# A load moved behind two transposes, and another held until one of them has landed, in a linear-attention and feed-forward kernel

## The chip, the cores and the metric

The kernel runs on one core of a Trainium2 chip. The metric is the device time of one execution in microseconds (us). Before the change it is 257.47 us, the median of three runs (256.48 to 258.15).

The engines of the core are named as in the profile: PE (TensorE; PEld is its weight load), DVE (VectorE), ACT (ScalarE), POOL (GpSimd) and SP (SyncE). Each engine works through its own instructions in the order of the program. An instruction waits at its place for the semaphores that it needs, and everything behind it on the same engine waits with it. In this kernel SP and POOL hardly compute: they issue DMAs, SP the loads of whole blocks, the transposes and the stores, POOL the weights, some early loads and the short tails of q, k and v. An issue is not a landing: a DMA is handed to a queue, and lands when its data have been moved.

## The reference

The input is q, k and v with 8 batches, 8 heads, 576 positions and 64 dimensions, in f32, and the four matrices of a feed-forward part.

```python
def phi(x):
    return np.where(x > 0, x, np.exp(x) - 1.0) + 1.0
q_p, k_p = (phi(q), phi(k))
kv = np.einsum('bhsd,bhse->bhde', k_p, v)
z = np.sum(k_p, axis=2)
num = np.einsum('bhsd,bhde->bhse', q_p, kv)
den = np.einsum('bhsd,bhd->bhs', q_p, z)[..., None] + 1e-06
attn = (num / den).astype(np.float32)

x = attn.transpose(0, 2, 1, 3).reshape(B * S, H * D)     # 4608 x 512
a = x @ w1                                               # 512 x 1024
b = x @ w2                                               # 512 x 1024
h = a * b @ w3                                           # 1024 x 1024
out = h @ w_out                                          # 1024 x 512
```

## The kernel before, in words

The attention of a batch is worked in the 512 positions that make four tiles of 128 (`NJ = 4`) and a tail of 64 (`R`). Blocks of q, k and v of one batch are loaded in two halves of four heads each, 512 KB a half. The two last matrices are multiplied with each other at the start, into `wf_sb`, so that a batch's feed-forward part is two products with w1 and w2, an elementwise product, and one product with `wf_sb`.

The whole order of the work is written out by hand in a string, `ORDER`, that `step` reads token by token. A token is a letter, the batch, and a part; a `+` at its end chooses another engine. Those that matter here are:

- `L`, `M`, `N`: load half a block of k, q, v (`load_qkv`, line 105, on SP here). The blocks take turns in 13 buffers of one pool, in the order of the tokens. `R`: load the tails of q and k (part 0: four DMAs of 64 KB) or of v (part 1: two DMAs), line 114, on POOL with a `+`.
- `x`, `y`, `z` for k and `X`, `Y`, `Z` for q: the exponential on ACT (line 178), max(x, 0) + 1 on DVE (line 183) and the minimum of the two on DVE (lines 203 and 208), which is phi. The result for k is `kj`, for q `qj`, and both tails go behind `qj` in one tile.
- `v`: cast half a block of v (line 214) or its tail (line 220) to bf16, on ACT, DVE or POOL.
- `K`: `kv_full`, the products of phi(k) with v and with ones into `kvp` on PE (lines 238 to 248), copied to `kv` (line 253).
- `T`: `qt_load`, a DMA on SP that transposes all of a batch's phi(q) and its tails, 18 blocks of 128 x 128 (line 268).
- `A`: `nat`, the product of transposed phi(q) with kv on PE (line 299), and on DVE the division into `xn` (lines 303 to 305). `D`: `xt_load`, a DMA on SP that transposes a batch's `xn`, 16 blocks, into `xt` (line 330).
- `F`: `f_unit`, for one of eight column blocks the products of x with w1 and with w2 (line 341), copied out by ACT (line 346) and multiplied by DVE (line 347). They use four PSUM banks (`mm_ps`), two for a unit.
- `O`: `o_unit`, eight products with `wf_sb` (line 498) and a copy of the result (line 500). `S`: the store of two of them, 512 KB, on SP (line 508).

A number behind a letter is the batch and the part: `L4.0` is the first half of k of batch 4, `T3.0` the transpose of q of batch 3, `D2.0` that of x of batch 2, `K3` the k-v products of batch 3.

Batches overlap: while PE computes the feed-forward part of batch 2, the attention of batch 3 is made ready, and the blocks of batch 4 and 5 are loaded. The loads run far ahead of their use, and the queue of SP holds many of them at a time. A DMA on SP or POOL also waits for the landing of the DMA that is eight before it on the same engine, since eight semaphores take turns.

Loads can be ordered against one another by `GATES`, a string that is empty before the change. `step` keeps the last DMA of each load under its token in `held`, and a token that stands on the left of a `<` in `GATES` waits until the DMA held under the token on the right has landed (`loaded` and `after`):

```python
def loaded(s, ins):
    s = s.rstrip("+")
    if s in gates:
        after(ins, held[gates[s]])
    held[s] = ins
```

The functions that the diff touches, and what calls them:

Of the kernel before, what the change touches and what calls it, by code (L numbers as in the profile page):

```python
# [13 lines left out]
P = 128  # L14
# [6 lines left out]
def kernel(  # L21
# [11 lines left out]
    nc = tc.nc  # L33
# [58 lines left out]
    raw, held = {}, {}  # L92
# [16 lines left out]
    def load_tail(b, part, alt):  # L109
        names = ("qk", "v")[part]  # L110
        t = raw[names + "r", b] = ldr.tile([P, len(names), RW], F32, tag="ldr" + names, name=names + "32r")
        for i, name in enumerate(names):
            for g in range(2):
                ins = (nc.gpsimd if alt else nc.sync).dma_start(  # L114
                    out=t[g * R:(g + 1) * R, i].rearrange("p (h d) -> p h d", d=D),
                    in_=src[name][b, g * 4:(g + 1) * 4, NJ * P:S, :].rearrange("h p d -> p h d"))
        return ins

    WQ = 256

# [135 lines left out]
    NB = KC * NJ  # L256

    def qt_tile(b):
        if (b, 0) not in qts:
            t = qts[b] = att.tile([P, NB + 2, P], BF16, tag="qt", name="qt")  # L260
            qts[b, 0] = t[:, 0:NB].rearrange("p (c j) t -> p c (j t)", j=NJ)
            qts[b, 1] = t[:, NB:NB + 2]
        return qts[b]

    def qt_load(b, part):
        t, s = qt_tile(b), ph["qt", b]
        i = NB if part else 0
        nc.sync.dma_start(out=t[:, i:NB + 2], in_=s[:, i * P:(NB + 2) * P], transpose=True)

    def q_tr(b, g, alt):  # L270
        qj, _ = ph["q", b]
# [77 lines left out]
    def f_unit(c, f):  # L349
        a_ps, b_ps = f_open(c, f)  # L350
        for ps, w in ((a_ps, w1_sb), (b_ps, w2_sb)):
            for kc in range(KC):
                f_mm(c, f, ps, w, kc)
        f_close(c, f, a_ps, b_ps)
# [4 lines left out]
    def ws_make(w, i, alt):  # L359
        t, s = (w1_sb, w2_sb)[w], wss[w]  # L360
        s[i] = ws_p.tile([P, 2, NQ * P], BF16, tag=f"w{w}{i}", name=f"ws{w}{i}")

        def blk(r, h):
            return t[:, 2 * h:2 * h + 2, r * NCH:r * NCH + NQ * P]
        a, b, op = ((lambda: blk(1, 0), lambda: blk(1, 1), ALU.add),
                    (lambda: s[0], lambda: blk(0, 0), ALU.subtract),
                    (lambda: blk(0, 0), lambda: blk(1, 0), ALU.subtract),
                    (lambda: blk(0, 1), lambda: s[1], ALU.subtract))[i]
        (nc.gpsimd if alt else nc.vector).tensor_tensor(out=s[i], in0=a(), in1=b(), op=op)

    def xs_make(c, i, alt):
        if c not in xss:
            xss[c] = xt_p.tile([P, 4, 2, 2, P], BF16, tag="xs", name="xs", bufs=1)
        x, s = xt_of(c), xss[c]

        def blk(h, r):
            return x[:, 2 * r:2 * r + 2, 2 * h:2 * h + 2]
        a, b = ((lambda: blk(0, 1), lambda: blk(0, 0)), (lambda: blk(1, 1), lambda: s[:, 0]),
                (lambda: blk(1, 1), lambda: blk(0, 1)), (lambda: blk(1, 0), lambda: s[:, 1]))[i]
        (nc.gpsimd if alt else nc.vector).tensor_tensor(  # L380
            out=s[:, i], in0=a(), in1=b(), op=ALU.subtract)
# [19 lines left out]
    def g_unit(c, q, i):  # L401
        if c not in abs_:
            abs_[c] = ab_p.tile([P, FC, NCH], BF16, tag="ab", name="ab")
        st = cs_.setdefault((c, q), {})
        a, m, name, first = ((), ((0, 0, 0), (0, 0, 0), "u", True), ((0, 0, 1), (0, 1, 0), "t", True),
                             ((1, 1), (1, 1), "u", False), ((1, 0), (1, 0), "t2", True),
                             ((1, 2), (1, 2), "u", False), ((1, 3), (0, 1, 1), "t2", False),
                             ((0, 1, 1), (1, 3), "u", False))[i]
        if first:
            pool, tag = (o_ps_p, "ou"[q % 2]) if name == "u" else (mm_ps, "mm")  # L410
            st[name] = pool.tile([P, 2, HN], F32, tag=tag, name="g" + name)
        t = st[name]
        g_product(t, c, q, a, m, first)
        if i in (1, 3, 4):
            s = st["s", i] = fsm("gs")
            nc.scalar.copy(out=s, in_=t)
        elif i in (2, 5, 6):
            s = st["c", i] = fsm("gc")
            nc.vector.tensor_tensor(out=s, in0=st["s", {2: 1, 5: 4, 6: 3}[i]], in1=t, op=ALU.add)
        else:  # L420
            s = fsm("ga")
            nc.scalar.copy(out=s[:, 0], in_=t[:, 0])
            nc.vector.tensor_mul(out=abs_[c][:, q + 4, 0:HN], in0=s[:, 0], in1=t[:, 1])

    def g_mul(c, q, i, alt):
        s = cs_[c, q]["c", i]
        f, r = {2: (q, 0), 5: (q + 4, 1), 6: (q, 1)}[i]
        (nc.gpsimd if alt else nc.vector).tensor_mul(
            out=abs_[c][:, f, r * HN:(r + 1) * HN], in0=s[:, 0], in1=s[:, 1])
# [64 lines left out]
    def o_unit(c, m, alt):  # L494
        ab = abs_[c]
        o_ps = o_ps_p.tile([P, DM], F32, tag="ou"[m % 2], name="o_ps")
        for f in range(FC):
            nc.tensor.matmul(o_ps, ab[:, f, m * P:(m + 1) * P], wf_sb[:, f, :],  # L498
                             start=(f == 0), stop=(f == FC - 1))
        copy_of(alt)(out=rows_of(c, m // 2)[:, m % 2], in_=o_ps)  # L500
# [45 lines left out]
    R2.0+ h0 h1 A0.4 P1.1+ Y2.1 h2 h3 R3.0+ M3.1 i0 A1.4 M2.0 i1 x2.1 X3.1 Z2.1 F1.7 F1.6 x2.2 L2.0  # L546
    y2.1 y2.2 Y2.0 x3.2 R3.1+ X2.0 O0.3 N2.1 x2.0 z2.1 N2.0 y2.0 z2.2 Z2.0 F1.0 M3.0 R5.0+ y3.2 T2.0
    v2.1 L3.0 Y3.1 R2.1+ F1.5 N3.1 v2.0+ z2.0 L3.1 Z3.1 v2.2+ O0.2 F1.2 F1.1 Y3.0 y5.2 z3.2 K2 F1.4
    A2.2 X3.0 F1.3 L4.0 A2.3 x3.0 O0.1 Z3.0 A2.0 x3.1 N3.0 y3.0 O0.0 v3.1 S0.1 A2.1 y3.1 R5.1+ z3.0
    z3.1 v3.0 v3.2 O1.1+ O1.0 T3.0 D2.0 S0.0 K3 R4.1+ R4.0+ O1.3 A3.0 O1.2 A3.2 L4.1 v4.2+ F2.6 A3.3  # L550
    F2.3 N4.1 y4.1 F2.1 M4.0 x4.1 A3.1 x4.0 F2.0 M4.1 y4.2 M6.1 v5.2+ x4.2 F2.7 Y4.0 D3.0 F2.4 z4.1
    X4.1 F2.2 Y4.1 v4.1 S1.0 F2.5 Z4.1 M5.0 N4.0 X4.0 Z4.0 A3.4 z4.2 y4.0 O2.3 F3.7 M5.1 Y5.0 v4.0
    A2.4 F3.6 z4.0 L5.0 T4.0 R6.0+ x5.2 Y5.1 X5.0 F3.1 N5.1 Z5.0 S1.1 O2.2+ K4 F3.2 M6.0 x6.2 X5.1
# [8 lines left out]
    F7.7 F7.2 F8.0 S6.1 F8.7 S6.0 F8.1 F8.5 F7.4 F8.2 F8.4 F7.6 O8.2 F7.5 H8.2 F7.3 F7.0 O8.3 H8.3  # L562
    O7.0 O7.1 S7.0 O8.0 O8.1 S8.0 O7.2 H7.2 Q7.3
    """
    GATES = ""
    ctx.enter_context(tc.manual_schedule())
    gates = dict(g.split("<") for g in GATES.split())

# [6 lines left out]
    def step(s):  # L575
        alt = len(s) - len(s.rstrip("+"))
        op, *at = s.rstrip("+").replace(".", " ").split()
        b = int(op[1:]) if op[1:] else None
        i = int(at[0]) if at else None
        t = op[0]  # L580
        if t == "F":
            f_unit(b, i)
        elif t == "G":
            g_unit(b, i, int(at[1]))
        elif t == "m":
            g_mul(b, i, int(at[1]), alt)
        elif t == "e":
            ws_make(b, i, alt)
        elif t == "d":
            xs_make(b, i, alt)  # L590
        elif t == "O":
            o_unit(b, i, alt)
        elif t == "V":
            w_unit(b, i)
        elif t == "s":
            s_make(b, i, alt)
        elif t == "S":
            o_store(b, i)
        elif t == "H":
            o_store(b, i // 2, i % 2)  # L600
        elif t == "Q":
            o_last(b, i)
        elif t == "I":
            constants(b, alt)
        elif t == "w":
            w3_tr(b, alt)
        elif t == "u":
            wf_mm(b, i, alt)
        elif t == "t":
            wt_make(b)  # L610
        elif t in "LMN":
            name = "kqv"["LMN".index(t)]
            loaded(s, load_qkv(name, b, i, alt))
        elif t == "R":
            loaded(s, load_tail(b, i, alt))
        elif t == "B":
            loaded(s, load_w12(b, i))
        elif t == "C":
            loaded(s, load_wo(b))
        elif t == "E":  # L620
            loaded(s, load_w3(b))
        elif t in "xX":
            phi_exp("kq"["xX".index(t)], b, i)
        elif t in "yY":
            phi_max1("kq"["yY".index(t)], b, i, alt)
        elif t in "zZ":
            phi_min("kq"["zZ".index(t)], b, i)
        elif t == "v":
            v_unit(b, i, alt)
        elif t == "T":  # L630
            qt_load(b, i)
        elif t == "a":
            q_tr(b, i, alt)
        elif t == "K":
            kv_full(b, alt)
        elif t == "A":
            nat(b, i)
        elif t == "D":
            xt_load(b, i)
        elif t == "P":  # L640
            xt_tr(b, i, alt)
        elif t == "h":
            if b == 0:
                held["h"] = [f_open(0, 0), f_open(0, 1)]
            for f in range(2):
                for ps, w in zip(held["h"][f], (w1_sb, w2_sb)):
                    f_mm(0, f, ps, w, b)
        elif t == "i":
            f_close(0, b, *held["h"][b])
# [32 lines left out]
```

## Time and profile before

| What | us |
|---|---|
| median of three runs | 257.47 |
| the profiled execution | 255.3 |
| its span, from the first to the last instruction | 253.5 |
| PE busy in it | 231.9 |
| DVE busy | 156.9 |
| ACT busy | 116.3 |
| POOL busy | 48.9 |

The granted clock of TensorE is 0.997 of full speed over the span. The DMA engines are at or near full use in nearly all of the first two thirds of the span, and hardly used in most of the last third; 38.80 MB are read from HBM and 9.44 MB written.

The profile is one execution. Its span is shorter than the execution's own time by what lies before the first and after the last instruction. Times in the views are microseconds from the start of the span. In a timeline, a row gives the start, the length, the engine, the line, the operation, the tiles as out<-in, their shapes and the number of instructions merged; in brackets stands the idle time of the engine before it and what ended it. A `q` behind an engine's name is its sequencer, which issues a DMA: the length is that of the issue, not of the transfer. The times to landing come from the list of DMA issues.

### The profile page before, as it was taken

What the parts mean: (1) busy time and instruction counts of PE and PEld (TensorE: products, weight loads), DVE (VectorE), ACT (ScalarE), POOL (GpSimd) and SP (SyncE); (2) the same over time, 40 slices, a digit from 0 to 9 for tenths busy, and PEclk for the clock granted to TensorE, in tenths of its full rate; (3) what the DMA queues carried; (4) which work ended last, traced back from release to release, by engine and by line L of the source; (5) the groups of instructions that cost most, each with busy time, mean ns of one, the idle gap of its engine ahead of it and who ended that gap; (6) DMA issues with size and microseconds to landing.
All of it is one profiled execution on the core that took longest, in us unless ns stands there. A gap on an engine that the chain in (4) does not pass through costs nothing.

```text
span 253.5 us, 3863 instructions
## 1 busy us (share of the span) xinstructions
PE 231.9 (91%) x1400; PEld 118.1 (47%) x1400; DVE 156.9 (62%) x350; ACT 116.3 (46%) x179; POOL 48.9 (19%) x82
## 2 busy tenths in 40 slices
PE   0088999999999789999999999999999999999994
PEld 0064564654454444445445545454544444444442
DVE  0548498679988546897987899878235632442300
ACT  2402676357756518738472573645332322333231
POOL 8524469446154100600000000000000000000000
PEclk9999999999999999999999999999999999999998
DMA  6999999999999999899999989646611244000144
GB/s 213 216 226 217 293 271 182 194 278 296 279 253 284 243 244 354 182 299 238 346 295 257 299 214 269 155 92 151 204 23 67 98 84 168 0 0 0 41 147 145
DMA packets 65427, 49.54 MB, mean 195 GB/s; under 512 B 33536, under 2 KB 60416, under 8 KB 65408
## 3 DMA queue, kind: packets, MB, share of 16 engines
q1 hardware_dynamic: 54576, 37.10, 56.7%
q0 software_dynamic: 10688, 12.06, 23.7%
q8 instruction: 11, 0.18, 0.3%
q10 hardware_dynamic: 144, 0.13, 0.1%
q14 instruction: 8, 0.07, 0.1%
HBM read 38.80 MB, written 9.44 MB: 190 GB/s over the span
## 4 chain that ended last, share of the span: by engine, by line
PE 75%; DMA 20%; POOL 1%; issue 1%; ACT 1%; ACTq 0%; POOLq 0%
PE a_ps L341 24%; PE b_ps L341 24%; PE o_ps L498 20%; DMA w3b<-in_moe_w_dram 10%; DMA out_dram<-o_sb 5%; PE nd L299 3%; DMA qk32r<-in_k_dram 3%; DMA xt<-xn 2%; PE kvp L244 2%; PE o_ps L523 1%; PE kvp L248 1%; PE kvp L238 0%; POOL w3b L136 0%; ACT e L178 0%; PE xtp L320 0%
## 5 line engine op out<-in xcount | busy, mean ns | idle before, releaser
L341 PEld LDWEIGHTS <-w_sb 128*128 128x128 bf16 x576 | 55.2, 98 | 63.0 <-issue 1.6
L347 DVE TENSOR_TENSOR ab<-a_sb,b_ps 128x512 bf16<-128x512 f32 x72 | 49.3, 685 | 39.4 <-PE b_ps L341 31.1
L341 PE MATMUL a_ps<-xt,w_sb 128*128 128x512 bf16 x256 | 66.7, 379 | 1.4 <-DMA xt<-xn 0.8
L346 ACT COPY a_sb<-a_ps 128x512 f32<-128x512 f32 x72 | 41.9, 585 | 56.1 <-PE a_ps L341 51.7
L341 PE MATMUL b_ps<-xt,w_sb 128*128 128x512 bf16 x256 | 66.7, 379 | 0.0
L498 PE MATMUL o_ps<-wf_sb,ab 128*128 128x512 bf16 x280 | 64.4, 379 | 0.0
L498 PEld LDWEIGHTS <-ab 128*128 128x128 bf16 x280 | 26.8, 98 | 30.0
L500 ACT COPY o_sb<-o_ps 128x512 f32<-128x512 f32 x29 | 16.9, 585 | 40.6 <-PE o_ps L498 28.2
L305 DVE TENSOR_TENSOR xn<-nd,r 128x512 bf16<-128x512 f32 x32 | 22.1, 691 | 1.1
L178 ACT ACTIVATE e<-q 128x1024 bf16<-128x1024 f32 x16 | 16.7, 1054 | 6.2 <-DMA q<-in_q_dram 6.2
L178 ACT ACTIVATE e<-k 128x1024 bf16<-128x1024 f32 x16 | 16.6, 1055 | 5.3 <-DMA k<-in_k_dram 5.3
L146 PE MATMUL w3p<-ident,w3b 128*128 128x128 bf16 x64 | 5.7, 242 | 13.5 <-DMA w3b<-in_moe_w_dram 13.5
L299 PEld LDWEIGHTS <-qt 128*128 128x128 bf16 (+1 forms) x160 | 11.5, 99 | 11.4 <-issue 2.7
L183 DVE TENSOR_SCALAR y<-q 128x1024 bf16<-128x1024 f32 x16 | 11.1, 700 | 8.2 <-DMA q<-in_q_dram 8.2
L299 PE MATMUL nd<-kv,qt 128*128 128x130 bf16 (+1 forms) x160 | 15.8, 220 | 0.5 <-ACT kv L253 0.5
L153 PE MATMUL wf_ps<-wt_sb,w3t 128*128 128x512 bf16 x64 | 15.1, 379 | 0.6 <-DMA wt_sb<-in_moe_w_out_dram 0.6
L303 DVE TENSOR_SCALAR r<-nd 128x8 f32<-128x8 f32 (+1 forms) x40 | 6.4, 161 | 12.6 <-PE nd L299 12.2
L114 POOL DMA_DIRECT2D qk32r<-in_q_dram x14 | 9.3, 674 | 16.9 <-ACT a_sb L346 14.8
L208 DVE TENSOR_TENSOR qj<-e,y 128x512 bf16<-128x512 bf16 x32 | 11.9, 416 | 0.4 <-ACT e L178 0.3
L208 DVE TENSOR_TENSOR kj<-e,y 128x512 bf16<-128x512 bf16 x32 | 11.9, 417 | 0.2
L146 PEld LDWEIGHTS <-w3b 128*128 128x128 bf16 x64 | 4.5, 108 | 15.0 <-DMA w3b<-in_moe_w_dram 14.8
L114 POOL DMA_DIRECT2D v32r<-in_v_dram x12 | 7.6, 640 | 18.1 <-DVE vr L220 8.1
(59 smaller groups left out, 185.0 us busy)
## 6 DMA issues: line engine op xcount, KB each, us to landing
out_dram<-o_sb SPq DMA_DIRECT2D x15, 512.0 KB, 3.8
q<-in_q_dram SPq DMA_DIRECT2D x13, 512.0 KB, 7.9
k<-in_k_dram SPq DMA_DIRECT2D x13, 512.0 KB, 6.3
v<-in_v_dram SPq DMA_DIRECT2D x12, 512.0 KB, 8.9
w3b<-in_moe_w_dram POOLq DMA_DIRECT2D x8, 256.0 KB, 12.2
w_sb<-in_moe_w_dram POOLq DMA_DIRECT2D x8, 256.0 KB, 7.3
q<-in_q_dram POOLq DMA_DIRECT2D x3, 512.0 KB, 11.4
k<-in_k_dram POOLq DMA_DIRECT2D x3, 512.0 KB, 12.4
```

The source lines that it names most:

```text
L114: ins = (nc.gpsimd if alt else nc.sync).dma_start(out=t[g * R:(g + 1) * R, i].rearrange("p (h d) -> p h d", d=D), in_=src[name][b, g * 4:( ...
L153: nc.tensor.matmul(wfs[i], w3ts[i][:, kc, :], wo_sb[:, kc, :], start=(kc == 0), stop=(kc == FC - 1))
L178: nc.scalar.activation(out=e, in_=x, func=AF.Exp)
L183: (nc.gpsimd if alt else nc.vector).tensor_scalar(out=y, in0=x, scalar1=0.0, scalar2=1.0, op0=ALU.max, op1=ALU.add)
L208: nc.vector.tensor_tensor(out=p[0][:, 2 * g + c].rearrange("p j u d -> p u j d"), in0=e[:, c], in1=y[:, c], op=ALU.min)
L299: nc.tensor.matmul(nd[rows, g, i * 2 * E1:(i + 1) * 2 * E1], w, kvs[b % 2][:, i, g].rearrange("p u e -> p (u e)"), start=True, stop=True)
L305: nc.vector.tensor_tensor(out=dst.rearrange("p (g h) e -> p g h e", g=2), in0=v4[:, :, :, 0:D], in1=r[rows].unsqueeze(3).to_broadcast([n, ...
L341: nc.tensor.matmul(ps, w[:, kc, f * P:(f + 1) * P], xt_of(c)[:, :, kc, :], start=(kc == 0), stop=(kc == KC - 1))
L346: nc.scalar.copy(out=a_sb, in_=a_ps)
L347: nc.vector.tensor_mul(out=abs_[c][:, f, :], in0=a_sb, in1=b_ps)
L498: nc.tensor.matmul(o_ps, ab[:, f, m * P:(m + 1) * P], wf_sb[:, f, :], start=(f == 0), stop=(f == FC - 1))
L500: copy_of(alt)(out=rows_of(c, m // 2)[:, m % 2], in_=o_ps)
```

## The change

Three things change.

- In `ORDER`, `L4.0` moves from before `A2.3` to behind `S0.0`. On SP it is issued behind `N3.0`, `S0.1`, `T3.0`, `D2.0` and `S0.0` and not ahead of them. The other tokens keep their order; on PE, DVE, ACT and POOL no instruction moves. Since the buffers of blocks are given out in the order of the tokens, `L4.0` and `N3.0` exchange theirs.
- `GATES` holds one entry, `R6.0<T3.0`: the tails of q and k of batch 6, loaded on POOL, wait for the landing of the transpose of q of batch 3. For that `step` keeps the DMA that `qt_load` now returns.
- `load_tail` returns the first of its DMAs and no longer the last, so that a gate holds the first of them, and with it those behind it on the same engine.

```diff
@@ load_tail
         t = raw[names + "r", b] = ldr.tile([P, len(names), RW], F32, tag="ldr" + names, name=names + "32r")
+        first = None
         for i, name in enumerate(names):
             for g in range(2):
                 ins = (nc.gpsimd if alt else nc.sync).dma_start(
                     out=t[g * R:(g + 1) * R, i].rearrange("p (h d) -> p h d", d=D),
                     in_=src[name][b, g * 4:(g + 1) * 4, NJ * P:S, :].rearrange("h p d -> p h d"))
-        return ins
+                first = first or ins
+        return first
@@ qt_load
-        nc.sync.dma_start(out=t[:, i:NB + 2], in_=s[:, i * P:(NB + 2) * P], transpose=True)
+        return nc.sync.dma_start(out=t[:, i:NB + 2], in_=s[:, i * P:(NB + 2) * P], transpose=True)
@@ ORDER
-    A2.2 X3.0 F1.3 L4.0 A2.3 x3.0 O0.1 Z3.0 A2.0 x3.1 N3.0 y3.0 O0.0 v3.1 S0.1 A2.1 y3.1 R5.1+ z3.0
-    z3.1 v3.0 v3.2 O1.1+ O1.0 T3.0 D2.0 S0.0 K3 R4.1+ R4.0+ O1.3 A3.0 O1.2 A3.2 L4.1 v4.2+ F2.6 A3.3
+    A2.2 X3.0 F1.3 A2.3 x3.0 O0.1 Z3.0 A2.0 x3.1 N3.0 y3.0 O0.0 v3.1 S0.1 A2.1 y3.1 R5.1+ z3.0 z3.1
+    v3.0 v3.2 O1.1+ O1.0 T3.0 D2.0 S0.0 L4.0 K3 R4.1+ R4.0+ O1.3 A3.0 O1.2 A3.2 L4.1 v4.2+ F2.6 A3.3
@@
-    GATES = ""
+    GATES = "R6.0<T3.0"
@@ step
         elif t == "T":
-            qt_load(b, i)
+            held[s] = qt_load(b, i)
```

## The prediction

> **What bounds the kernel now.** I read the page's first two parts, then every idle stretch of PE in the timeline, then who ended it, and last the SP and POOL queues in front of those two places. PE is busy for 231.9 of 253.5 us:
>
> ```profile
> PE 231.9 (91%) x1400; PEld 118.1 (47%) x1400; DVE 156.9 (62%) x350; ACT 116.3 (46%) x179; POOL 48.9 (19%) x82
> ```
>
> Its idle time lies in the first 40.6 us, with two exceptions. The timeline of PE (start, length, instruction, idle time before it and its releaser in brackets):
>
> ```profile
> 83.78 1.89 PE L498 MATMUL o_ps<-wf_sb,ab 128*128 128x512 bf16 x8
> 87.10 0.61 PE L244 MATMUL kvp<-vt,kj 128*128 128x130 bf16 x8 [1.43 <-ACT vt L214]
> 87.84 0.27 PE L248 MATMUL kvp<-vr,qj 128*128 128x260 bf16 x1
> ...
> 93.37 1.02 PE L341 MATMUL a_ps<-xt,w_sb 128*128 128x512 bf16 x4 [0.79 <-DMA xt<-xn]
> ```
>
> The first is K3, which waits 1.43 us for batch 3's v, and 0.13 us more for its tail (87.10 + 0.61 = 87.71 to 87.84). The second is F2.6, which waits 0.79 us for D2.0, the transpose of batch 2's x. Together 2.35 us; after 93.4 PE never waits again, so whatever ends sooner there ends the kernel sooner, as long as nothing behind it becomes late.
>
> Who holds these two? ACT's timeline, and the chain that ended last (start, length, what; for a DMA from issue to landing):
>
> ```profile
> 82.51 1.05 ACT L214 CAST vt<-v 128x1024 bf16<-128x1024 f32 x1
> 86.00 1.05 ACT L214 CAST vt<-v 128x1024 bf16<-128x1024 f32 x1 [2.43 <-DMA v<-in_v_dram]
> ```
>
> ```profile
> 74.23 13.31 DMA out_dram<-o_sb
> 87.53 5.79 DMA xt<-xn
> ```
>
> ACT casts one half of v at 82.51 and then waits 2.43 us for the other half, N3.0. The store S0.1, ready at 74.23, lands only at 87.6: the queue is backed up. SP's timeline shows in which order:
>
> ```profile
> 72.24 1.00 SPq L105 DMA_DIRECT2D k<-in_k_dram  x2
> 73.34 0.80 SPq L105 DMA_DIRECT2D v<-in_v_dram  x1
> 74.23 1.15 SPq L508 DMA_DIRECT2D out_dram<-o_sb  x1
> 80.54 6.90 SPq L268 DMA_TRANSPOSE qt<-qj  x1
> 87.53 1.87 SPq L330 DMA_TRANSPOSE xt<-xn  x1
> ```
>
> These are L3.0 and L4.0 (k of batches 3 and 4), N3.0, S0.1, T3.0, D2.0. By their times to landing they land at 79.3, 82.7, 86.0, 87.6, 89.6 and 93.3. T3.0's issue alone holds SP for 6.90 us, until S0.1 has landed, and D2.0 cannot be issued before.
>
> **L4.0 moved behind T3.0, D2.0 and S0.0.** It took 82.7 - 79.3 = 3.4 us of queue ahead of N3.0. It adds and removes no instruction; on SP it passes N3.0, S0.1, T3.0, D2.0 and S0.0. N3.0 takes its place and its buffer and lands at about 82.7, just after ACT begins the other half. Then ACT casts 83.5 to 84.5 and the tail to 85.4; DVE finishes kj at 83.90 + 1.42 = 85.3; PE is free for K3 at 87.10 - 1.43 = 85.67. So **K3 loses its 1.56 us**; the next latest is kj, 0.35 us ahead.
>
> S0.1 follows at about 84.4 (it took 1.6 us), T3.0, whose operands were there at 80.54, 2.0 us behind it as before, at 86.4. D2.0 needs xn, which DVE ends at 82.70 + 0.69 = 83.4, and SP, which T3.0 frees at 84.4; 1.9 us of issue and 2.4 more (137.5 for D4.0, whose issue ended at 135.1 with no POOL load beside it) give 88.7; 1.5 us more, as D2.0 had beside two POOL loads, 90.2. PE, 1.56 us earlier, asks for it at 91.0. **F2.6 loses its 0.79 us**, with a cover of 0.8 to 2.3 us.
>
> L4.0 itself, behind S0.0, lands near 92 to 94; its first reader x4.0, ACT's second of two exponentials from 98.72 on, would now be due near 97.4. L4.1 in front of it in use has less: today 96.3 for an x4.1 at 98.72; then about 88.7 + 1.9 + 1.5 + 1.3 = 93.4, and up to 96.6 if all six POOL loads of R6.0 and R6.1 go beside it, against a need of 96.4. If that cover is gone, ACT is late by some tenths, which the four mm banks (two units of 1.7 us) take up. I cost it at nothing. The buffer that L5.1 and N5.0 get is exchanged too; both owners are read before 113, those loads are issued at 118.5 and later: nothing.
>
> **R6.0 gated behind T3.0, and held on its first DMA.** Of R6.0's four POOL DMAs the first now waits for T3.0's landing. They were issued from 76.52 to 80.6 and landed at 84.0 to 87.6, beside N3.0, S0.1 and T3.0's start; now they go at about 86.4 to 88.9. Behind them on POOL stand only R6.1 (88.08, by its own wait) and R7.0 (102.92): R6.1 slips by about 1 us, R7.0 not at all. R6.0's reader is ACT's tail exponential at 119.84, R6.1's a cast at 148.32: covers of 25 us and more. What the gate is worth I bound by zero and by four times what such a 64 KB piece costs the SP queue: between 79.3 and 86.0 two 512 KB loads took 6.7 us instead of 3.0 (1.5 each at 97.8 to 100.8), with seven pieces landing among them, so 0.52 us each, 2.1 us in all. For K3 and F2.6 it is worth nothing more, since both waits are gone by the load alone. At worst it is a loss of the same 2.1 us, behind D2.0.
>
> **What is late next.** PE 2.35 us earlier meets K4. The timelines of ACT, DVE and PE:
>
> ```profile
> 113.96 1.05 ACT L214 CAST vt<-v 128x1024 bf16<-128x1024 f32 x1 [2.50 <-DMA v<-in_v_dram]
> 114.91 0.58 ACT L346 COPY a_sb<-a_ps 128x512 f32<-128x512 f32 x1
> ```
>
> ```profile
> 115.52 0.69 DVE L347 TENSOR_TENSOR ab<-a_sb,b_ps 128x512 bf16<-128x512 f32 x1 [1.03 <-ACT a_sb L346]
> 116.13 0.75 DVE L208 TENSOR_TENSOR kj<-e,y 128x512 bf16<-128x512 bf16 x2
> ```
>
> ```profile
> 117.17 0.62 PE L244 MATMUL kvp<-vt,kj 128*128 128x130 bf16 x8
> ```
>
> N4.0 lands at 113.94; ACT casts it, then copies a_sb, on which DVE waits, and DVE ends kj at 116.88, 0.29 us before K4 takes it. This chain starts at a landing, not at PE, so it moves only as far as N4.0. In front of N4.0 stand M6.1 (102.2), D3.0 (105.75), S1.0 and M5.0. The queue moves the same bytes from 79.3 to M6.1 in either order, so M6.1 stays near 102.2. But D3.0, issued at 101.47 once DVE had written A3.1's xn (101.44), landed 3.5 us behind M6.1, where a transpose that stands ready behind a full queue lands 2.0 (T3.0, T4.0) to 2.5 us (D4.0) behind. With PE and DVE 2.35 us earlier it stands ready: N4.0 comes 1.0 to 1.5 us earlier, I take 1.3. K4 then waits 2.35 - 0.29 - 1.3 = 0.76 us. Behind K4 the covers are wider: T4.0 118.8 for a nat at 120.02, T5.0 135.0 for 137.60, D4.0 137.5 for 139.78, each growing by the same 1.3.
>
> **Sum:** 0.76 - 1.56 - 0.79 = -1.6 us. The profiled execution took 255.3 us, so 253.7; the median of the three runs is 257.47 (256.48 lowest), 2.2 above the profiled one, and I carry the difference over: **255.9**.
>
> **The rivals.**
> 1. *All 2.35 us stay.* There is a hole at 86 to 87, in which the DMA engines moved 33 GB/s. If it closes too, N4.0 comes over 2.06 us earlier and K4 does not wait: 255.1. Against it: T4.0 started behind ordinary loads, without POOL pieces, with no better landing than 2.0 us.
> 2. *Given back at K4.* The transfers are the same, so N4.0 lands at 113.94 as before, and only K4's 0.29 us remains: 257.2. For it: DMA shares near 1 from 74 to 102. The Trainium skill says in "DMA: Bandwidth & Descriptors", Issuing engines are not separate DMA queues, that DMAs of all issuing engines run on the same 16 engines and interleave; by that rule a new order makes no capacity, and the sum is this rival's. The slowed loads of 79 to 86 agree with it; D3.0's late operand, a wait of the order and not of capacity, is why I don't follow it whole.
> 3. *Slower.* R6.0 and R6.1, six pieces released at T3.0's landing, fall on D2.0, which took 3.8 us behind T3.0 beside two pieces and 2.5 (D4.0) beside none: 0.65 each, so 2.5 + 6 x 0.65 = 6.4 us after 86.4, at 92.8, and with its old place nearly regained nothing is won by F2.6. L4.0 (1.5 us) and R6.0 (2.1) are now between D2.0 and N4.0, which lands at 117.5; K4 waits 3.6 - 0.29 = 3.3 us: 260.8. It decides from N4.0 landing after 114.2. Against it: the two pieces issued at 88.08 landed at 92.5 and 93.2, together with D2.0's end and not ahead of it. The skill's same page, Queues, rings and completion order, has each engine take turns between queue rows packet by packet, which speaks for this rival; the two pieces of 88.08 neither show nor exclude it.
> 4. *The change does not reach T3.0:* something other than the queue holds its issue until 87.4, and N3.0 keeps its landing: 257.5. Only N3.0 at 86.0 again would show it.
>
> **How the numbers follow.** Forecast 0.42, rival 1 0.22, rival 2 0.18, rival 3 0.13, rival 4 0.05. One per cent, 2.6 us, is about what a measurement of this kernel can tell from no change. The waits in the trace come to 2.35 us, so faster by over 1% needs runs that wait longer there than the profiled one: 0.13, out of rival 1 and the forecast's edge. Slower by over 1% is rival 3 and its neighbourhood: 0.14. Same: 0.73. The range runs from 254.7 (rival 1, less scatter) to 258.0 (rivals 2 and 4, plus scatter), and leaves out rival 3.
>
> **What would show it.** In the changed profile: no PE wait before the kvp near 85.7; ACT's second v cast right behind the first; T3.0's issue ending near 84.4; D2.0 landing before 91; a PE wait of some 0.8 us at K4 near 115, ended by DVE's kj, with ACT waiting for v ahead of it; POOL's R6.0 issued at T3.0's landing. I am wrong if D2.0 lands after 91, if N4.0 lands after 113, or if another wait of PE appears between 93 and 162, where the DMA queues are full.

## The result, and the profile after

| What | before, us | after, us |
|---|---|---|
| median | 257.48 (256.48 to 258.15, 6 runs) | 254.74 (253.79 to 255.72, 6 runs) |
| ratio, with its 95% interval | | 0.990 (0.9865 to 0.9935) |
| the profiled execution | 255.3 | 254.38 |
| its span | 253.5 | 252.6 |

The rows of the table say different things: the medians are 2.7 us apart, the two profiled executions 0.9. The forecast, 255.9, is 1.2 us above the median. Medians here are over all executions of a kernel, while the ratios leave out those that took over 1.5% longer than the fastest of the same kernel, so a ratio is not the quotient of two medians. Below, the 0.9 is read from the two traces first, and then the rest is looked for.

In the code most lines stand two further down after the change; the load of blocks is still at 105, and the tails are at 115. PE is as busy as before; a few of its records are missing from this trace. The busy times in the page after the change:

```profile
PE 231.3 (92%) x1384; PEld 117.8 (47%) x1400; DVE 156.9 (62%) x350; ACT 116.1 (46%) x179; POOL 48.7 (19%) x82
```

The two places of the prediction, and two new ones, in PE's timeline after the change (start, length, engine, instruction; in brackets the idle time before it and its releaser):

```profile
85.32 0.62 PE L246 MATMUL kvp<-vt,kj 128*128 128x130 bf16 x8
...
90.35 1.03 PE L343 MATMUL a_ps<-xt,w_sb 128*128 128x512 bf16 x4
...
98.97 1.02 PE L343 MATMUL b_ps<-xt,w_sb 128*128 128x512 bf16 x4 [0.23 <-DVE ab L349]
100.15 1.02 PE L343 MATMUL a_ps<-xt,w_sb 128*128 128x512 bf16 x4 [0.16 <-ACT a_sb L348]
...
116.28 0.63 PE L246 MATMUL kvp<-vt,kj 128*128 128x130 bf16 x8 [0.88 <-DVE kj L210]
```

K3 at 85.32 and F2.6 at 90.35 follow the matmul before them without a wait: the 2.35 us are gone. K4 begins at 116.28, against 117.17 before, so only 0.89 us of them are left there; 0.88 is waited at K4 itself, and 0.39 at 98.97 and 100.15. The first two places are cured by ACT's two casts of v, now back to back, and by a shorter issue of T3.0. ACT's timeline after the change, and then SP's (a `q` behind the engine means an issue):

```profile
82.32 2.00 ACT L216 CAST vt<-v 128x1024 bf16<-128x1024 f32 x2
...
97.63 2.00 ACT L180 ACTIVATE e<-k 128x1024 bf16<-128x1024 f32 x2 [1.94 <-DMA k<-in_k_dram]
99.54 0.57 ACT L348 COPY a_sb<-a_ps 128x512 f32<-128x512 f32 x1
...
113.64 1.05 ACT L216 CAST vt<-v 128x1024 bf16<-128x1024 f32 x1 [1.90 <-DMA v<-in_v_dram]
114.59 0.58 ACT L348 COPY a_sb<-a_ps 128x512 f32<-128x512 f32 x1
```

```profile
73.16 0.45 SPq L105 DMA_DIRECT2D v<-in_v_dram  x1
73.70 0.72 SPq L510 DMA_DIRECT2D out_dram<-o_sb  x1
80.34 4.47 SPq L270 DMA_TRANSPOSE qt<-qj  x1
84.91 2.98 SPq L332 DMA_TRANSPOSE xt<-xn  x1
87.98 0.53 SPq L510 DMA_DIRECT2D out_dram<-o_sb  x1
88.61 1.41 SPq L105 DMA_DIRECT2D k<-in_k_dram  x2
```

T3.0's issue ends at 84.81 instead of 87.44, and D2.0 is handed over behind it at once. The other waits are explained by ACT's lines and by these of DVE:

```profile
97.63 0.69 DVE L185 TENSOR_SCALAR y<-k 128x1024 bf16<-128x1024 f32 x1 [1.90 <-DMA k<-in_k_dram]
98.24 0.68 DVE L349 TENSOR_TENSOR ab<-a_sb,b_ps 128x512 bf16<-128x512 f32 x1
...
115.20 0.69 DVE L349 TENSOR_TENSOR ab<-a_sb,b_ps 128x512 bf16<-128x512 f32 x1 [1.13 <-ACT a_sb L348]
115.80 0.75 DVE L210 TENSOR_TENSOR kj<-e,y 128x512 bf16<-128x512 bf16 x2
```

L4.1 lands at 97.60 (96.29 before). DVE's y4.1 waits 1.90 us for it and does the product `ab`, for which PE waits at 98.97, only behind that; ACT's x4.1 waits 1.94 us for it, and the copy `a_sb`, for which PE waits at 100.15, comes only behind the two exponentials. N4.0 lands at 113.61 (113.94 before). ACT's cast of it waits 1.90 us, the copy `a_sb` stands behind the cast, DVE waits for that copy, and `kj` comes behind DVE's product: K4 waits for `kj`.

The gate is visible in POOL's timeline after the change:

```profile
88.44 1.23 POOL L115 DMA_DIRECT2D qk32r<-in_q_dram  x2 [11.87 <-DMA qt<-qj]
89.66 1.22 POOL L115 DMA_DIRECT2D qk32r<-in_k_dram  x2
90.87 1.22 POOL L115 DMA_DIRECT2D v32r<-in_v_dram  x2
```

R6.0 and R6.1 are released by T3.0's landing (87.87) and issued together from 88.44 to 92.1, so all six pieces move beside L4.0 and L4.1: L4.0 lands at 94.43, L4.1 at 97.60, and the pieces between 94.73 and 99.00, three of them ahead of L4.1.

### The profile page after: what moved, and what is told of

The parts are those of the page before. It is cut to its first block, busy times and chain, and to the rows that moved or that the text cites. A ratio compares the mean times of both kernels' runs of the same rounds, so it can differ in the third digit from the quotient of the medians.

```text
span 252.6 us, 3848 instructions
## 1 busy us (share of the span) xinstructions
PE 231.3 (92%) x1384; PEld 117.8 (47%) x1400; DVE 156.9 (62%) x350; ACT 116.1 (46%) x179; POOL 48.7 (19%) x82
## 4 chain that ended last, share of the span: by engine, by line
PE 69%; DMA 21%; issue 3%; SPq 2%; DVE 2%; POOL 1%; ACT 1%; ACTq 0%; POOLq 0%
PE a_ps L343 21%; PE b_ps L343 21%; PE o_ps L500 20%; DMA w3b<-in_moe_w_dram 10%; DMA q<-in_q_dram 5%; DMA v<-in_v_dram 3%; PE nd L301 3%; DMA qk32r<-in_k_dram 3%; PE kvp L246 2%; SPq L105 1%; SPq L332 1%; PE o_ps L525 1%; DVE kj L210 1%; PE kvp L250 1%; PE kvp L240 0%
## 5 line engine op out<-in xcount | busy, mean ns | idle before, releaser
L500 PE MATMUL o_ps<-wf_sb,ab 128*128 128x512 bf16 x267 | 62.7, 379 | 0.8 <-issue 0.2
L155 PE MATMUL wf_ps<-wt_sb,w3t 128*128 128x512 bf16 x61 | 14.8, 379 | 0.7 <-DMA wt_sb<-in_moe_w_out_dram 0.5
L185 DVE TENSOR_SCALAR y<-k 128x1024 bf16<-128x1024 f32 x16 | 11.0, 687 | 2.0 <-DMA k<-in_k_dram 1.9
L148 PEld LDWEIGHTS <-w3b 128*128 128x128 bf16 x64 | 4.5, 109 | 14.8 <-DMA w3b<-in_moe_w_dram 14.5
```

Source lines behind the costliest of these rows:

```text
L148: nc.tensor.transpose(tp[:, kc, :], raw["w3", i // 4][:, i % 4, kc * P:(kc + 1) * P], ident)
L155: nc.tensor.matmul(wfs[i], w3ts[i][:, kc, :], wo_sb[:, kc, :], start=(kc == 0), stop=(kc == FC - 1))
L185: (nc.gpsimd if alt else nc.vector).tensor_scalar(out=y, in0=x, scalar1=0.0, scalar2=1.0, op0=ALU.max, op1=ALU.add)
```

## The experiments

The table holds what the experiments are read from: landings in us, taken from the list of DMA issues, PE's waits between 60 and 160 us of the timeline, and the span of that execution. "M6.1's place" and "N4.0's place" are the places in SP's queue, whichever of the two loads stands there. "T4.0 behind L5.0" is the landing of a transpose less that of the load in front of it.

| Kernel | gate | N3.0 | D2.0 | S0.1 to D2.0 | M6.1's place | D2.0 to there | N4.0's place | T4.0 behind L5.0 | PE waits | span |
|---|---|---|---|---|---|---|---|---|---|---|
| before | no | 85.98 | 93.33 | 5.71 | 102.22 | 8.90 | 113.94 | 1.95 | 2.4 | 253.5 |
| before, second (e1) | no | 86.41 | 94.09 | 6.43 | 104.64 | 10.55 | 115.37 | 1.98 | 3.3 | 254.7 |
| before, third (e8) | no | 86.56 | 95.21 | 6.83 | 103.98 | 8.77 | 116.12 | 1.98 | 4.5 | 257.1 |
| load moved, no gate (e2) | no | 82.10 | 90.58 | 6.71 | 103.11 | 12.54 | 111.89 | 1.97 | 0.9 | 251.8 |
| the same, second (e12) | no | 83.14 | 92.20 | 6.20 | 104.48 | 12.28 | 113.49 | 1.96 | 1.2 | 252.5 |
| the same, M6.1 and N4.0 exchanged (e7) | no | 82.31 | 91.13 | 6.08 | 103.53 | 12.41 | 112.13 | 1.94 | 0.7 | 251.3 |
| N3.0 and L4.0 exchanged (e9) | no | 82.71 | 93.00 | 5.25 | 103.92 | 10.91 | 114.04 | 1.94 | 2.7 | 254.6 |
| after | yes | 82.66 | 89.62 | 4.68 | 104.44 | 14.81 | 113.61 | 1.97 | 1.4 | 252.6 |
| after, second (e11) | yes | 82.76 | 90.17 | 4.58 | 105.22 | 15.05 | 114.62 | 1.98 | 2.6 | 253.6 |
| after, M6.1 and N4.0 exchanged (e6) | yes | 83.17 | 89.93 | 4.60 | 106.20 | 16.27 | 114.96 | 1.93 | 2.5 | 253.8 |
| after, R7.0 held too (e4) | yes | 82.27 | 89.25 | 4.56 | 105.51 | 16.26 | 113.28 | 3.90 | 2.9 | 253.7 |
| gate alone (e3) | yes | 86.42 | 92.21 | 4.53 | 106.34 | 14.14 | 114.60 | 1.96 | 2.6 | 254.0 |
| load moved, gate behind M6.1 (e10) | late | 82.41 | 89.35 | 4.59 | 101.92 | 12.57 | 111.75 | 6.16 | 6.1 | 259.7 |

Span less PE's waits is 251 us, within 0.4, in every row but three: e9, e10 and the third of before. Those hold 3.4, 6.8 and 3.4 us at half the granted clock; half of that, without the parts in which PE waits anyway (0.47 in e9, 0.91 in e10), is 1.5, 3.0 and 1.7 us. With these taken off too they come to 250.4, 250.6 and 250.9. So the span of this kernel is a fixed stretch of about 251 us, and on top of it what PE waits for and what the clock loses. The waits of 60 to 160 us are not all at K3, F2.6 and K4: 0.43 us of the second profile of before stands at 70.66, and 0.70 of e2 lies at 147.2 and 148.5, both on a copy by ACT.

### The load alone, and the gate alone

The changed kernel without its gate:

```diff
-    GATES = "R6.0<T3.0"
+    GATES = ""
```

> The load L4.0 moved, no gate. Theory A (the load ahead of N3.0 makes both waits, the gate adds nothing to them): N3.0 lands near 82.7, no wait at K3, D2.0 before 91, time as the changed kernel, ratio 0.988 to 0.992. Rival (the gate makes the difference, by keeping R6.0's pieces away from T3.0): T3.0 lands 1 to 2 us later than with the gate, F2.6 waits 0.5 us or more, ratio 0.994 or above.

Measured: 254.53 us (253.33 to 254.85, 8 runs), ratio 0.9897 (0.9862 to 0.9932). The moved load alone gives all that the whole change gives. N4.0 lands at 111.89 and K4 does not wait. F2.6 in PE's timeline of this kernel waits 0.1 us, for D2.0, which landed at 90.58:

```profile
90.62 1.02 PE L343 MATMUL a_ps<-xt,w_sb 128*128 128x512 bf16 x4
```

The changed kernel with L4.0 back in its old place:

```diff
-    ... F1.3 A2.3 x3.0 ...
+    ... F1.3 L4.0 A2.3 x3.0 ...
-    ... T3.0 D2.0 S0.0 L4.0 K3 ...
+    ... T3.0 D2.0 S0.0 K3 ...
```

> The gate R6.0 behind T3.0, the load L4.0 in its old place. Theory A: the two waits stay, a little shorter, since N3.0 has two or three 64 KB pieces fewer beside it (1 to 1.5 us of queue): K3 waits 0.3 to 0.8 us, and R6.0 behind T3.0 meets D2.0 as before: ratio 0.994 to 1.002. Rival (the gate makes the difference): ratio 0.992 or below, no wait at K3.

Measured: 256.29 us (253.71 to 258.99, 12 runs), ratio 0.9958 (0.9923 to 0.9993): a gain of about 1 us, as far as this can be told from no change. PE's timeline of this kernel:

```profile
87.54 0.61 PE L246 MATMUL kvp<-vt,kj 128*128 128x130 bf16 x8 [1.45 <-ACT vt L216]
...
110.31 1.04 PE L343 MATMUL a_ps<-xt,w_sb 128*128 128x512 bf16 x4 [0.84 <-DMA xt<-xn]
```

K3 waits as before, since its v still lands at 86.42. F2.6's wait is gone, because the gate brings D2.0 to 4.53 us behind S0.1 (5.71 to 6.83 in the three profiles of before). But PE now waits 0.84 us for D3.0, the next transpose of x: the six pieces land between 96.89 and 102.41, in front of M6.1, which lands at 106.34. The table shows the same exchange in all kernels with this gate: 4.5 to 4.7 us from S0.1 to D2.0, 5.3 to 6.8 without; and with the load moved, 14.8 to 16.3 us from D2.0 to M6.1's place, 12.3 to 12.5 without. Where the load is moved, the gate saves 1.4 to 2.2 us at one transpose and spends 2.3 to 4.0 behind it: M6.1's place lands at 103.7 on the mean of the three profiles without the gate, and at 105.3 on that of the four with it.

### The kernels before and after once more

The change of the median was larger than all waits of the first profile, 2.35 us. So the kernel before was profiled again, without an edit.

> The kernel before, unchanged, profiled once more. The profile of before shows 255.3 us and 2.35 us of PE waits behind 40.6 us (K3 1.56, F2.6 0.79); its other runs took 256.5 to 258.15, and the change moved the medians by 2.74 us where the two profiles differ by 0.9. Theory A (the first profile was an execution with short waits): this one takes about 257.5 and its PE waits at K3 and F2.6 are 3.5 to 5 us together. Rival (the difference lies elsewhere, at the start or the end of the span): waits at K3 and F2.6 again near 2.3 us, whatever the time.

> The kernel before, profiled a third time. The first profile (255.3 us) had 2.35 us of PE waits behind 40.6 us, the second (256.43) 3.2. If the medians' 2.7 us against the profiles' 0.9 come from executions in which T3.0 and D2.0 land later, this one, at the usual 257, has 3 us or more at K3, at the nat behind T3.0 and at F2.6, with T3.0 landing over 3 us behind S0.1. If the difference lies elsewhere: waits as in the first, 2.3 us.

Measured: 256.43 and 258.83 us (255.3 in the first profile). The medians of the kernel before, taken beside the experiments on three chips, are 257.28, 257.35 and 257.39, so the chip is not the reason. The second execution waits 3.3 us on PE:

```profile
87.53 0.61 PE L244 MATMUL kvp<-vt,kj 128*128 128x130 bf16 x8 [1.47 <-ACT vt L214]
...
91.43 0.40 PE L299 MATMUL nd<-kv,qt 128*128 128x130 bf16 x4 [0.60 <-DMA qt<-qj]
...
94.13 1.02 PE L341 MATMUL a_ps<-xt,w_sb 128*128 128x512 bf16 x4 [0.35 <-DMA xt<-xn]
```

At K3, with its tail, and F2.6 these are 1.95 us, less than in the first profile; with the wait for T3.0, which landed 3.73 us behind S0.1, they are 2.55. So this execution speaks for the rival of its expectation and not for longer waits at the two places. The third waits 4.5 us:

```profile
87.68 0.61 PE L244 MATMUL kvp<-vt,kj 128*128 128x130 bf16 x8 [2.23 <-ACT vt L214]
...
95.25 1.02 PE L341 MATMUL a_ps<-xt,w_sb 128*128 128x512 bf16 x4 [1.97 <-DMA xt<-xn]
...
97.77 1.91 PE L341 MATMUL a_ps<-xt,w_sb 128*128 128x512 bf16 x4
...
100.61 1.03 PE L341 MATMUL a_ps<-xt,w_sb 128*128 128x512 bf16 x4
```

Both waits are the ones of the prediction, K3 and F2.6, but 2.23 and 1.97 us long and not 1.43 and 0.79. T3.0 landed 2.06 us behind S0.1 here, not over 3 as was expected; what is late is D2.0, at 95.21. And behind the waits four matmuls at 97.77 take 1.91 us, where the same four take 1.03 at 100.61. The table of stretches of this kernel (stretch and length; busy time and count of PE, PEld, DVE, ACT, POOL; granted clock, DMA share, GB/s) shows why:

```profile
96.00:98.00 2.00, 2.00 (x11) 1.02 (x9) 0.00 (x0) 0.77 (x2) 0.00 (x0) 0.65 1.09 330
98.00:100.00 2.00, 2.00 (x6) 0.68 (x5) 1.11 (x4) 1.07 (x3) 0.00 (x0) 0.50 1.10 349
100.00:102.00 2.00, 2.00 (x11) 0.93 (x10) 1.67 (x3) 0.64 (x2) 0.00 (x0) 1.00 1.10 349
```

The granted clock is halved from about 96.6 to 100.0 (0.65 in the first stretch is full speed for 0.6 us and half for 1.4). So the third execution is 3.53 us longer than the first: 2.0 of longer waits at K3 and F2.6, and 1.7 from the clock.

The two kernels with the load moved were run again in the same way.

> The changed kernel again, on the chip of the next one, to compare gate and no gate side by side. Theory A (the gate adds nothing): ratio 0.988 to 0.992, and within 0.003 of the kernel without it. Rival (the gate saves on top): 0.003 or more below it.

> L4.0 moved, no gate, beside the last. Theory A: ratio 0.988 to 0.992, within 0.003 of the changed kernel. Its profile: T3.0 to D2.0 late as before the change (S0.1 to D2.0 in 5.7 to 6.7 us where the gated kernels take 4.5 to 4.7), and N4.0 1 to 2 us earlier than with the gate. Rival: 0.003 or more above the changed kernel.

Measured: the changed kernel 255.72 us (253.58 to 257.7, 12 runs), ratio 0.9938 (0.9904 to 0.9972); without the gate 255.08 us (252.97 to 260.97, 6 runs), ratio 0.9899 (0.984 to 0.9959). The second profile of the changed kernel has the same two new waits as the first, longer:

```profile
100.00 1.02 PE L343 MATMUL b_ps<-xt,w_sb 128*128 128x512 bf16 x4 [0.86 <-DVE ab L349]
...
117.28 0.63 PE L246 MATMUL kvp<-vt,kj 128*128 128x130 bf16 x8 [1.22 <-DVE kj L210]
```

The second one without the gate waits elsewhere, at K3's successor for T3.0 and at F2.6 for D2.0, which land later without it:

```profile
89.19 0.40 PE L301 MATMUL nd<-kv,qt 128*128 128x130 bf16 x4 [0.47 <-DMA qt<-qj]
...
92.24 1.02 PE L343 MATMUL a_ps<-xt,w_sb 128*128 128x512 bf16 x4 [0.70 <-DMA xt<-xn]
```

The three profiled executions without the gate (e2, e7, e12) have spans of 251.3 to 252.5 us, those of the changed kernel 252.6 and 253.6. The timed intervals overlap, so whether the gate costs half a microsecond or nothing is left open; that it brings a gain beside the moved load is not seen in any run. The gain that it has alone (e3) does not add to that of the load.

### N3.0 alone given its place

In the kernel before, only L4.0 and N3.0 exchanged:

```diff
-    ... F1.3 L4.0 A2.3 ... x3.1 N3.0 y3.0 ...
+    ... F1.3 A2.3 ... x3.1 N3.0 L4.0 y3.0 ...
```

> The kernel before, with N3.0 issued ahead of L4.0 and nothing else: L4.0 stays ahead of S0.1, T3.0 and D2.0, and there is no gate. Theory A (two separate waits on one queue, and the load must leave the way of both): N3.0 lands near 82.5, K3 does not wait; D2.0 still lands at 93 to 94, so F2.6 waits for all that K3 won, 2 to 2.5 us; ratio 0.997 to 1.002. Rival (K3's wait for v is what costs, and F2.6's wait goes with it): F2.6 waits under 1 us, ratio 0.993 or below.

Measured: 258.55 us (12 runs, eleven of them 256.48 to 259.92), ratio 1.0042 (1.0009 to 1.0074), a little above what was expected. The twelfth, the profiled one, took 318.22 us, with a granted clock of 0.75 from 18.6 us on to the end, and shows nothing of the waits. A second profile:

> N3.0 ahead of L4.0 and nothing else, profiled once more, since the first profile of it fell into a throttled execution. Theory A: N3.0 lands near 82.5 and K3 does not wait; D2.0 lands at 93 to 95 and F2.6 waits 2 to 3.5 us in one piece. The granted clock, if one long wait makes TensorE slow down: a stretch at 0.5 behind F2.6, as the third profile of before has it. Rival: F2.6 waits under 1 us, or the clock stays at 1.00 behind a wait of over 2 us.

The second profile took 256.41 us. PE's timeline in it:

```profile
85.11 0.62 PE L244 MATMUL kvp<-vt,kj 128*128 128x130 bf16 x8
...
88.59 2.61 PE L498 MATMUL o_ps<-wf_sb,ab 128*128 128x512 bf16 x8 [2.18 <-DVE o_sb L500]
91.67 0.62 PE L299 MATMUL nd<-kv,qt 128*128 128x130 bf16 x4 [0.47 <-DMA qt<-qj]
```

and DVE's:

```profile
87.84 0.69 DVE L500 COPY o_sb<-o_ps 128x512 f32<-128x512 f32 x1 [2.91 <-DMA out_dram<-o_sb]
```

N3.0 lands at 82.71, as early as in the changed kernel, and K3 does not wait. But PE then waits 2.18 us for a PSUM bank, which DVE frees late because its copy needs the buffer that the store S0.1 reads until 87.75. The load that stands in front of S0.1 makes somebody late either way: the gain needs L4.0 behind S0.1, not only behind N3.0. Whether it must stand behind the two transposes too, no run shows: a place between S0.1 and T3.0 was not tried. The expectation had the kind right and named the wrong place, F2.6; D2.0 landed at 93.00, in time for a PE that late.

### Where the gate's bytes go

Three kernels ask what the wait at K4 hangs on. In the first, the tails of batch 7 also wait, for N4.0:

```diff
-    GATES = "R6.0<T3.0"
+    GATES = "R6.0<T3.0 R7.0<N4.0"
```

> The changed kernel, with the tails of batch 7 (R7.0, and R7.1 behind it on POOL, six pieces of 64 KB) held until N4.0 has landed. Theory A (K4 gives back 0.88 us because N4.0 lands late in a full queue, and those pieces are in front of it): N4.0 lands 1.5 to 3 us earlier, K4 does not wait, about 0.9 us less than the changed kernel: ratio to before 0.985 to 0.988. Rival (N4.0 is late by the order on SP alone, the pieces fill holes): N4.0 within 0.5 us of 113.6, K4 waits 0.6 us or more, ratio 0.989 to 0.991.

Measured: 255.63 us (254.22 to 257.63, 12 runs), ratio 0.9952 (0.9921 to 0.9983). N4.0 lands only 0.33 us earlier than after the change and not 1.5 to 3, K4 still waits 0.42, and a new wait stands at the next product of q:

```profile
115.95 0.63 PE L246 MATMUL kvp<-vt,kj 128*128 128x130 bf16 x8 [0.42 <-DVE kj L210]
...
120.21 0.40 PE L301 MATMUL nd<-kv,qt 128*128 128x130 bf16 x4 [1.23 <-ACT e L180]
```

The releaser is named as ACT, but this product needs T4.0, which landed at 120.16, 3.90 us behind L5.0. In the kernels with no pieces released there it is 1.93 to 1.98 each time. The pieces of batch 7 were issued from 113.85 on, in the middle of that transpose; four of them landed between L5.0 and T4.0.

In the second and the third, N4.0 takes M6.1's place in the queue, with the gate and without:

```diff
-    ... y4.2 M6.1 v5.2+ ... M5.0 N4.0 X4.0 ...
+    ... y4.2 N4.0 v5.2+ ... M5.0 M6.1 X4.0 ...
```

> The changed kernel with M6.1 and N4.0 exchanged on SP, the same bytes in the same places of the queue. Theory A (K4 gives back what N4.0's late landing costs): N4.0 lands near 104 in M6.1's place, ACT's cast of it does not wait, K4's wait of 0.88 us is gone, and the time is 0.5 to 0.9 us below the changed kernel's: ratio 0.986 to 0.989. Rival (another wait takes its place, T4.0 at the nat or D3.0): a PE wait of 0.5 us or more between 104 and 125, ratio 0.990 or above.

> As the last, without the gate: L4.0 moved, N4.0 in M6.1's place. If the gate is worth nothing: N4.0 near 103, no wait at K4, F2.6 waiting 0 to 0.5 us, ratio 0.986 to 0.989, the same as with the gate. If the gate matters for D2.0: F2.6 waits 0.5 us or more and the ratio is 0.003 above that with the gate.

Measured: with the gate 255.36 us (254.05 to 257.81, 12 runs), ratio 0.9929 (0.9895 to 0.9962); without it 254.68 us (253.09 to 255.91, 6 runs), ratio 0.9908 (0.9873 to 0.9942). With the gate K4's wait is gone, and others stand in its place:

```profile
100.24 1.02 PE L343 MATMUL b_ps<-xt,w_sb 128*128 128x512 bf16 x4 [1.38 <-DVE ab L349]
...
109.17 1.04 PE L343 MATMUL a_ps<-xt,w_sb 128*128 128x512 bf16 x4 [0.23 <-DMA xt<-xn]
...
119.95 0.40 PE L301 MATMUL nd<-kv,qt 128*128 128x130 bf16 x4 [0.39 <-DMA qt<-qj]
```

The first is again the wait for L4.1, which lands at 98.87. Without the gate one wait of a size that counts is left, 0.51 us at F2.6. So with the gate the time does not fall when N4.0 goes ahead; without it K4 does not wait in either order. This fits a queue that is late by the bytes that the gate put there, of which another owner pays if N4.0 does not.

Last, the gate of the changed kernel tied to M6.1:

```diff
-    GATES = "R6.0<T3.0"
+    GATES = "R6.0<M6.1"
```

> The changed kernel with R6.0 held until M6.1 has landed and not until T3.0 has: its four pieces and R6.1's two fall behind L4.0, L4.1, N4.1 and the q loads and not among them. Theory (the gate only carries the pieces to another place, and beside L4.0 and L4.1 they cost what they saved before D2.0): L4.1 lands near 94.5 and not 97.6, x4.1 does not wait, M6.1 lands near 100 to 101; D3.0 and N4.0 carry the pieces now and N4.0 lands at 111 to 113.5, so K4 waits 0 to 0.9 us; ratio 0.986 to 0.990. Rival (the pieces cost nothing where they are, L4.1 is late for another reason): L4.1 at 97 or later, ratio as the changed kernel's.

Measured: 261.56 us (259.74 to 263.61, 6 runs), ratio 1.0193 (1.0128 to 1.0257). Up to there it went as the theory has it: M6.1 landed at 101.92 and not 104.44, L4.1 at 96.04, and N4.0 at 111.75; PE waits 0.23 us at K4 and not at all for L4.1. Then comes this, in PE's timeline:

```profile
123.32 0.61 PE L301 MATMUL nd<-kv,qt 128*128 128x130 bf16 x4 [5.88 <-DMA qt<-qj]
```

POOL, held until 101.9, issues twelve pieces between 102.5 and 113.8, those of batch 6 and those of batch 7 that stood behind them. Eight of them land by 114.53, in front of L5.0 (117.12), and four between it and T4.0, which lands 6.16 us behind L5.0, at 123.28. In the table of stretches of this kernel the clock follows:

```profile
122.00:126.00 4.00, 2.68 (x10) 1.30 (x11) 1.73 (x5) 0.32 (x1) 0.00 (x0) 0.55 1.08 318
```

The clock is halved from 122.4 to 129.2. Waits and clock come to 6.1 + 3.0 us, against 1.4 in the profile of the changed kernel: 7.7 of difference, where the two executions are 7.1 us apart.

## Why the prediction was right and wrong

**K3 loses its 1.56 us: right.** N3.0 landed at 82.66 (predicted 82.7), ACT's casts stand back to back, and the wait is in none of the kernels that have N3.0 there and S0.1 behind it.

**F2.6 loses its 0.79 us: right, with smaller cover.** S0.1 landed at 84.94 (84.4), T3.0 at 87.87 (86.4, since it came 2.9 us behind S0.1 and not 2.0), D2.0 at 89.62, within 88.7 to 90.2. PE took it at 90.35, 0.7 us later; 0.8 to 2.3 were predicted. Without the gate the cover is gone, and 0.1 to 0.7 us of wait are left (e2, e7, e12).

**L4.0 and L4.1 "costed at nothing": mis-sized.** L4.1 landed at 97.60, above the 96.6 that was given for all six pieces beside it, against a need of 96.4. The way from D2.0 to L4.1 was sized rightly, 7.98 us against 4.7 and 3.2 for the pieces; it began 0.9 us late, since D2.0 landed at 89.62 and not at 88.7, the early end of its own range. And even the bound, 96.6, was past the need. The four mm banks took up only part: PE waited 0.39 us, and 1.02 in the second profile. The prediction looked at ACT alone; DVE's y4.1 waits for the same load.

**"The queue moves the same bytes ... so M6.1 stays near 102.2": true of the load, wrong of the gate.** M6.1 landed at 104.44, 2.2 us later than in the first profile of before, and N4.0 came 0.33 us earlier and not 1.3. The part behind M6.1 moved the right way and by more than was taken: from M6.1 to N4.0 it took 11.72 us before and 9.17 after. D3.0 stood ready, as was said, but landed 3.16 us behind M6.1 and not 2.0 to 2.5, since three pieces of R7.0 landed in between, which the prediction left out; in e10, where none did, it took 1.81. Over several profiles the effect on M6.1 is clearer: M6.1's place is at 103.6 before (mean of three), 103.7 with the load moved and no gate (three), 104.8 after the change (two); N4.0's place is at 115.1, 112.5 and 114.1. Moving the load does leave M6.1 where it was and brings N4.0's place 2.6 us forward, more than the sum had; the gate takes 1.6 of that back. SP's queue moves the same bytes, but POOL's does not: before, four pieces of R6.0 landed by 87.6, and after the change all six are issued behind 88.4. The chain from N4.0 to the cast, to a_sb, to ab, to kj and K4 was read rightly. That the wait there, 0.88 us, is near the predicted 0.76 is luck: N4.0 brought 1.0 us less than was taken, but PE had already lost 0.39 us on the way, and from N4.0's landing to K4 it was 2.67 us and not the 2.94 that the prediction has (3.23 less 0.29).

**The gate "for K3 and F2.6 worth nothing more ... at worst a loss of the same 2.1 us, behind D2.0": nearly right.** K3 needs nothing of it, F2.6 the 0.1 to 0.7 us above. Its cost behind D2.0 was in the bound, 2.1 us (measured, by the means above, 1.1 at M6.1's place and 1.6 at N4.0's), but the sum took it as nothing.

**The sum, -1.6 us: 0.9 in the pair of profiles.** Two of the prediction's own signs of being wrong came: N4.0 landed after 113, at 113.61, and PE waits at two new places between 93 and 162. PE waits 1.27 us at the new places (0.88 and 0.39) and not 0.76; that is 0.5 of the missing 0.7. For the other 0.2 the trace shows no wait, only a gap of 0.16 us at 106.00 in front of eight matmuls of which one has no record.

**"I carry the difference over": the step that made the forecast too high.** The 2.2 us between the profile and the median of before were taken as a constant of the measurement. The changed kernel's own difference is 0.4, and 0.3 in the second set of runs. The first profile of before was a short execution. What the longer ones lose is shown in part only: the third profile waits 4.33 us at K3 and F2.6 and loses 1.7 to the clock, the second waits 2.55 there and for T3.0, hardly more than the first. The prediction's own condition, that more than 1% "needs runs that wait longer there than the profiled one", is met by e8 and not by e1. The clock is the smaller part: of the 67 executions of before, those whose mean clock was 0.997 or more still have a median of 257.02 us, against 257.35 for all. So the median fell by 2.7 us where the argument had 1.6 and the two traces 0.9, and what makes up the rest stays open. The second measurement of the changed kernel gave 1.6 us (ratio 0.9938, 0.9904 to 0.9972), so the median itself is uncertain by about as much as it lies below the forecast. It lies at the very edge of the stated range, 254.7, and that edge came from rival 1, whose reason (K4 does not wait) the trace denies: that the range holds is partly luck.

**The rivals.** The first, that all 2.35 us stay, holds without the gate and not with it: in e2 N4.0 landed 2.05 us earlier and K4 did not wait. The second, that all of it is given back at K4, is wrong in its size, since 0.89 us remained there; of its reasoning this much was borne out, that the gate moved a cost and made no room. The Trainium skill's rule in "DMA: Bandwidth & Descriptors", Issuing engines are not separate DMA queues, that the DMAs of all engines share 16 DMA engines and interleave, agrees: what the gate saves up to D2.0, 1.4 to 2.2 us, it spends behind it, 2.3 to 4.0. The third, slower, did not happen at D2.0: the six pieces were issued from 88.44 on, behind most of it, and the first landed at 94.73. Its mechanism exists, and e10 shows it at T4.0, 6.16 us instead of 1.97 and 1.9% slower. The fourth is excluded: N3.0 landed at 82.66, and T3.0's issue fell from 6.90 to 4.47 us.

## What to carry to other kernels

In a queue that is full and kept in order, a load far ahead of its use is paid by whoever stands behind it; put it behind the transfers with the least slack, since passing only the first (e9) hands the delay to the next. Holding a transfer back removes no bytes: before a gate is added, look at what the held bytes, and all that stands behind them on the same engine, will land beside. And when a change takes away waits, take several profiles of the kernel before: its three spans lie between 253.5 and 257.1 us, and its waits between 2.4 and 4.5.

## What was not expected of the hardware

**A wait of 2 us can halve the clock for 3.4 us, or not, by where it falls.** The half-clock stretches begin a whole number of 3.41 us steps after the first moment at full clock. In the third profile of before that moment is 18.09 and the drop is at 96.59, 23 steps of 3.413 later; the step before it, 93.18 to 96.59, holds the wait of 1.97 us (58% of it). The longer wait of 2.23 us in the same execution, 85.45 to 87.68, is divided between two steps (0.9 and 1.3 us), and the clock stayed whole. In the profile of the exchanged loads (e9) the wait of 2.18 us lies in one step (64%), and the clock drops with the end of that step, at 89.6:

```profile
89.00:93.00 4.00, 3.53 (x14) 1.37 (x13) 0.60 (x3) 0.09 (x1) 0.00 (x0) 0.58 1.22 230
```

In the first profile of before 1.56 us lie in one step (46%), with no drop. In the thirteen profiles of the table no step at full clock in which PE was idle for 54% or less is followed by half clock, and each with 58% or more is, among them the last ones of the span, where PE runs out of work. In e10 the half clock lasted for two steps; in the first of them PE was idle for 0.91 us. Of 67 executions of the kernel before, 34 had a mean granted clock under 0.995 (median 257.69 us, the others 257.02), of 18 with the changed kernel none was under 0.997. That the share of one step decides is read from these cases and was not tested by itself.

The Trainium skill, "TensorE: Matmul & The Clock Gate", Part 1: The HAM clock gate (the "warmup" mystery), has a free-running window of 3413 ns, which agrees with the steps of 3.41 us, and half and full clock as its two states. The thirteen profiles show only these two, but the execution of 318.22 us was granted 0.75. The same part of the Trainium skill's page puts the fall to half behind at least one idle window of about 3.4 us; here windows that were 58% and 64% idle were enough.

**Small pieces of one queue cost a transpose of another more than their bytes would.** T4.0 lands 1.93 to 1.98 us behind L5.0 in eleven profiles, in which no piece of 64 KB lands in between. It lands 3.90 us behind in e4 and 6.16 in e10, and in both four pieces land in between. Four pieces are the bytes of half a 512 KB load, 0.75 us at the 1.5 us that such a load took alone; the transpose lost 1.9 and 4.2. D3.0, where its issue had ended by the landing of the load in front of it, lands 1.7 to 2.4 us behind that load with no piece in between, 2.8 to 2.9 with one or two, 3.2 with three (after the change) and 3.9 with five (e3). T3.0 and D2.0 together end 4.5 to 4.7 us behind S0.1 with no piece in between and 5.3 to 6.8 with three to five. Which property of the transfers does that, and why e4 and e10 differ, was not tested.
